# Fused attention and two gated layers on one core: reciprocals through a DRAM scratch, and a reordered gate in layer 1

## The chip, the cores and the metric

The kernel runs on one core of one Trainium2 chip. The metric is the device time of one execution in microseconds (us): the median of several runs of the same kernel. Lower is better.

## The reference

Pooled attention over 4 batches of 8 heads (1152 keys, 576 pooled queries, 64 columns each), then two feed-forward layers of 2304 tokens, 512 → 2048 → 512, each with its own gate:

```python
q_pool = q.reshape(B, H, S // 2, 2, D).mean(axis=3)
scores = scale * q_pool @ k^T;  scores -= max(scores)
attn = exp(scores);  attn = attn / (sum(attn) + 1e-9);  x = attn @ v
h = x @ w_in;   x = (h - tanh(h)) @ w_out           # layer 1
h = x @ w_in2;  out = (h / (1 + exp(-1.702 h))) @ w_out2   # layer 2
```

## The kernel before

Everything is fp32 accuracy from split operands: a value is a rounded high part and a low rest, and each product is three matmuls. The order of the work is written by hand (`tc.manual_schedule()`): every engine and the SP queue, which issues nearly all DMAs, run their instructions in the order in which the program emits them. Three stages follow each other.

**Attention** (`attention`, L185). The heads go in 16 pairs. A pair is 18 passes `i` = 0..17 of the loop over `g` (L479): nine key tiles of one head, then nine of the other. In one pass PE makes the scores `sc` (L320, L321), ACT takes two exponentials (`pf`, `ph`, L322, L324), DVE or POOL subtracts them (`pl`, L333), and PE, three passes later, adds to the output `pv` (L349). L321 needs a row of `q3` with the maxima of its queries. They are made one pair ahead: PE `mx` (L282), DVE reduce (L285), DVE transpose `tt` (L291) and four small DMAs `q<-tt` (L297, `max_rows`, pass 12). `stack` (passes 2 and 12) copies a head's operands in six DMAs, L271 to L276.

A finished head lies in `u` with its row of sums. `sums` (pass 4 of the next pair) brings the sums of a pair to 64 + 64 partitions (`s9`, L363, L365) and moves the second head under the first (L367). `recip` (pass 8): POOL L373, DVE reciprocal L375, then two DMAs (L378) that put the 576 reciprocals into one partition of `rb`, for each head. `spread` (pass 11): two DMAs (L387) copy that partition to the 63 below it. `normalise` (pass 16): DVE multiplies `u` by `rb` into the tokens `xb` (L397).

Weights are loaded to `raw` (L108, two buffers) and converted in three steps (`convert_steps`): s0 is ACT L121 and DVE L122, L126; s1 is DVE L133, L137; the split is ACT L144 and POOL L145. The table `when` (L406) sets the pass of each for the first weights: in the last pair `i` 3 is converted at passes 1, 2 and 4.

**Layers 1 and 2** (`moe`, L525) are 48 steps each: four quarters of the hidden width, six blocks of tokens, two halves `fp`. In step w PE makes `h` (24 matmuls, L550) and then the `y` of step w - 2 (L619); `gate` follows on ACT and DVE. `y` of `fp` 0 needs four PSUM banks, which come free when the previous `y` has been added to `xb`: by ACT copies (L630) in the first quarter, by DVE adds (L632) later, emitted between the gate's DVE operations. At the top of step w, `split_g(w - 1)` copies the gate's result to its high part (ACT L596) and takes the low rest (L598, on POOL in layer 1). Layer 1's gate is a polynomial in u = h² with a tanh branch, and a mask picks one:

```python
u = Square(h) (ACT L566); a = Square(u + GA0) (L567); d = tanh(h) (L568); e = Square(u + GB0) (L569)
g = GC*u*h (DVE L570); u = Relu(u - T2), the mask (ACT L572); d = h - d (DVE L574)
g = (a + GA1)*g (DVE L576); g = (e + GB1)*g (L579); copy d into g where the mask is set (L582)
```

`h` lies in PSUM, where ACT and DVE both read it; such reads of one PSUM tile are kept in the program's order. The table in `moe` (L648) gives the half-step of each later load and conversion.

Of the kernel before, what the change touches and what calls it, by code (L numbers as in the profile page):

```python
# [28 lines left out]
def tile_pooled_attention_two_moe(  # L29
# [31 lines left out]
    wpool = ctx.enter_context(tc.tile_pool(name="wpool", bufs=1))  # L61

# [122 lines left out]
    def attention(ctx: ExitStack):  # L185
# [174 lines left out]
        def sums(p):  # L360
            ua, ub = halves.pop(2 * p), halves.pop(2 * p + 1)
            s9 = wpool.tile([128, QJ], F32, tag="s9", name="s9", bufs=2)
            nc.sync.dma_start(  # L363
                out=s9[0:64, :], in_=ua[64:65, :].rearrange("o (p i) -> o p i", i=QJ))
            nc.sync.dma_start(  # L365
                out=s9[64:128, :], in_=ub[64:65, :].rearrange("o (p i) -> o p i", i=QJ))
            nc.sync.dma_start(out=ua[64:128, :], in_=ub[0:64, :])  # L367
            norm[p] = dict(ua=ua, s9=s9)

        def recip(p):  # L370
            s9 = norm[p]["s9"]
            r9 = wpool.tile([128, QJ], F32, tag="r9", name="r9", bufs=2)
            nc.gpsimd.tensor_scalar(  # L373
                out=r9, in0=s9, scalar1=1.0, scalar2=1e-9, op0=ALU.mult, op1=ALU.add)
            nc.vector.reciprocal(r9, r9)  # L375
            rb = wpool.tile([128, SP], F32, tag="rb", name="rb", bufs=1)
            for s in range(2):
                nc.sync.dma_start(  # L378
                    out=rb[64 * s:64 * s + 1, :].rearrange("o (p i) -> o p i", i=QJ),
                    in_=r9[64 * s:64 * s + 64, :])  # L380
            norm[p]["rb"] = rb

        def spread(p):
            rb = norm[p]["rb"]
            for s in range(2):
                row = rb[64 * s:64 * s + 1, :].unsqueeze(1)
                nc.sync.dma_start(  # L387
                    out=rb[64 * s + 1:64 * s + 64, :], in_=row.to_broadcast([1, 63, SP]))

        def normalise(p):  # L390
# [88 lines left out]
        for g in range(total + LAG):  # L479
# [43 lines left out]
        return lambda: (recip(last), spread(last)), lambda: normalise(last)  # L523

    def moe(ctx: ExitStack, ending):  # L525
# [30 lines left out]
        def gate(n, h, adds):  # L556

            g = temp("gg", 2)

            def add():  # L560
                if adds:
                    adds.pop(0)()

            if steps[n][0] == 0:
                u, a, e, d = temp("u"), temp("a"), temp("e"), temp("d")
                nc.scalar.activation(u, h, AF.Square)  # L566
                nc.scalar.activation(a, u, AF.Square, bias=GA0)  # L567
# [13 lines left out]
                add()
                nc.vector.copy_predicated(g, u[:].bitcast(I32), d)  # L582
            else:
                s = temp("a")
                nc.scalar.activation(s, h, AF.Sigmoid, scale=1.702)  # L585
                add()
                nc.vector.tensor_mul(g, h, s)
            gg[n] = g
            while adds:
                add()  # L590

        def split_g(n):
# [6 lines left out]
            gs[n] = gt  # L599

        def y_part(n):
# [35 lines left out]
            return [lambda m=m: add(m) for m in range(nm)]  # L637
# [24 lines left out]
        for w in range(len(steps) + YLAG):  # L662
            if 0 < w <= len(steps):
                split_g(w - 1)
# [6 lines left out]
            while adds:  # L671
                adds.pop(0)()
# [53 lines left out]
```

## Time and profile before

| what | us |
|---|---|
| median of 3 runs (1485.83 to 1492.15) | 1488.1 |
| the profiled execution | 1484.25 |
| its span, first to last instruction | 1482.4 |
| busy PE / DVE / ACT / POOL | 1343.8 / 1071.7 / 827.6 / 459.1 |

The profile is of one execution, 1.85 us of which lie outside the span. Shares of busy time are averages over three stages with different limits; the waits say more. A busy PE is not PE at its full clock.

### The profile page before, as it was taken

The page shows a single profiled execution, that of the slowest core. Times are in us where ns is not written, and L with a number is a line of the kernel's source. Part 1 is how long each engine was busy: PE and PEld are TensorE (multiplying, and loading weights), DVE is VectorE, ACT ScalarE, POOL GpSimd, SP SyncE. Part 2 cuts the span into 40 slices and gives each one's busy share as a digit, 9 for nine tenths or more (in the row PEclk, how much of TensorE's full clock was granted, in tenths as well). Part 3 has the DMA queues.
Part 4 walks back from the last instruction along what each step waited for, and adds up shares of the span by engine and source line. Part 5 has one row for each costly group of instructions (what it writes and reads, how often), then busy time and mean ns, then how long its engine had stood idle before and what let it go on. Part 6 is the DMA issues. An engine that isn't in the chain of part 4 may idle for free. (4 is left out here: it accounts for less than half of the span.)

```text
span 1482.4 us, 20903 instructions
## 1 busy us (share of the span) xinstructions
PE 1343.8 (91%) x7632; PEld 1262.8 (85%) x7632; DVE 1071.7 (72%) x1230; ACT 827.6 (56%) x1855; POOL 459.1 (31%) x344
## 2 busy tenths in 40 slices
PE   5998988887989797988998888988899999999998
PEld 4998888887989786878988888878899999999997
DVE  6886867777878787799789879889885345554433
ACT  2786767775868676576654555555654332222221
POOL 6554444443545445233322332232211010111000
PEclk9999999998999998999999999999999999999999
DMA  7756666666666564121001100101011101010011
GB/s 200 174 115 139 146 134 146 134 147 133 148 134 147 104 117 104 26 59 44 29 29 43 43 29 29 43 29 43 29 43 57 44 29 57 29 57 29 22 43 64
DMA packets 44038, 117.63 MB, mean 79 GB/s; under 512 B 11968, under 2 KB 11968, under 8 KB 43936
## 3 DMA queue, kind: packets, MB, share of 16 engines
q1 hardware_dynamic: 43900, 116.30, 32.4%
q8 instruction: 60, 0.98, 0.3%
q14 instruction: 42, 0.34, 0.1%
q10 hardware_dynamic: 36, 0.00, 0.0%
HBM read 61.87 MB, written 4.72 MB: 45 GB/s over the span
## 5 line engine op out<-in xcount | busy, mean ns | idle before, releaser
L322 ACT ACTIVATE pf<-sc 128x288 f32<-128x288 f32 x576 | 248.1, 432 | 147.6 <-PE sc L321 130.8
L324 ACT ACTIVATE ph<-sc 128x288 fp32r<-128x288 f32 x564 | 247.1, 438 | 0.0
L333 DVE TENSOR_TENSOR pl<-pf,ph 128x576 fp32r<-128x576 f32 x224 | 207.7, 948 | 41.0 <-ACT ph L324 35.7
L285 DVE TENSOR_REDUCE mt<-mx 128x1 fp32r<-128x1152 f32 x144 | 194.5, 1353 | 41.9 <-PE mx L282 41.7
L321 PE MATMUL sc<-q,a 65*128 65x288 f32 x576 | 172.8, 312 | 39.9 <-DMA q<-tt 39.9
L596 ACT ACTIVATE g<-gg 128x768 fp32r<-128x768 f32 x96 | 81.3, 847 | 209.5 <-DVE gg L582 156.7
L320 PE MATMUL sc<-q,a 128*128 128x288 f32 x576 | 173.6, 312 | 16.2 <-ACT pf L322 9.6
L598 POOL TENSOR_TENSOR g<-gg,g 128x768 fp32r<-128x768 f32 x48 | 91.9, 1916 | 273.3 <-ACT g L596 273.3
L321 PEld LDWEIGHTS sc<-q,a 65*128 65x128 f32 x576 | 115.4, 200 | 42.5 <-issue 32.1
L585 ACT ACTIVATE a<-h 128x768 f32<-128x768 f32 x48 | 39.0, 812 | 199.8 <-PE h L550 199.8
L632 DVE TENSOR_TENSOR xb<-xb,y 128x384 f32<-128x384 f32 (+1 forms) x126 | 76.0, 605 | 103.0 <-PE y L619 103.0
L349 PE MATMUL pv<-pl,vh 128*128 128x288 f32 x576 | 140.9, 309 | 8.2 <-DVE pl L333 4.6
L349 PE MATMUL pv<-ph,vh 128*128 128x288 f32 x576 | 140.9, 309 | 1.7
L349 PE MATMUL pv<-ph,vl 128*128 128x288 f32 x576 | 138.1, 304 | 0.0
L550 PE MATMUL h<-hl,w 128*128 128x384 f32 x720 | 131.4, 336 | 5.0 <-DVE hl L101 4.7
L320 PEld LDWEIGHTS sc<-q,a 128*128 128x128 f32 x576 | 115.5, 200 | 23.8 <-ACT ph L324 11.3
L550 PEld LDWEIGHTS h<-hl,w 128*128 128x128 f32 x720 | 125.6, 188 | 7.8 <-DVE hl L101 6.0
L282 PE MATMUL mx<-kh,bdq 128*128 128x384 f32 x432 | 112.8, 375 | 16.9 <-DVE mt L285 9.8
L333 POOL TENSOR_TENSOR pl<-pf,ph 128x576 fp32r<-128x576 f32 x64 | 103.6, 1618 | 63.1 <-ACT ph L324 52.3
L619 PE MATMUL y<-g,w 128*128 128x384 f32 x360 | 88.6, 355 | 23.5 <-DVE xb L632 15.2
L349 PEld LDWEIGHTS pv<-pl,vh 128*128 128x128 f32 x576 | 100.3, 198 | 11.1 <-DVE pl L333 5.7
L349 PEld LDWEIGHTS pv<-ph,vh 128*128 128x128 f32 x576 | 104.9, 200 | 5.2 <-ACT u L355 5.0
(114 smaller groups left out, 2908.4 us busy)
## 6 DMA issues: line engine op xcount, KB each, us to landing
a<-kh SPq DMA_DIRECT2D x64, 288.0 KB
raw<-in_moe_w_in_dram SPq DMA_DIRECT2D x32, 512.0 KB
raw<-in_moe_w_out_dram SPq DMA_DIRECT2D x32, 512.0 KB
qr<-in_q_dram SPq DMA_DIRECT2D x16, 576.0 KB
kr<-in_k_dram SPq DMA_DIRECT2D x16, 576.0 KB
vr<-in_v_dram SPq DMA_DIRECT2D x16, 576.0 KB
q<-qh SPq DMA_DIRECT2D x64, 144.0 KB
a<-kl SPq DMA_DIRECT2D x32, 288.0 KB
```

The costliest lines, as they stand in the source:

```text
L282: nc.tensor.matmul(mx[:, a, 0:384], bdqs[p % 2][:, j, :], d["kh"][:, a * 384:(a + 1) * 384], start=True, stop=True)
L285: nc.vector.tensor_reduce(d["mt"][:, j:j + 1], mx[:, :, 0:384], AX.XY, ALU.max, negate=True)
L320: nc.tensor.matmul(sc, a1[:, ks], q2[:, xs], start=True, stop=False)
L321: nc.tensor.matmul(sc, a2[:, ks], q3[:, xs], start=False, stop=True)
L322: nc.scalar.activation(pf[:, xs], sc, AF.Exp, scale=SCALE)
L324: nc.scalar.activation(ph[:, xs], sc, AF.Exp, scale=SCALE)
L333: eng.tensor_tensor(pl, pf, f32(ph[:]), op=ALU.subtract)
L349: nc.tensor.matmul(accs[hd][x], w[:, t, :], r[:, x * HB:(x + 1) * HB], start=(t == 0 and n == 0), stop=(t == KT - 1 and n == 2))
L550: nc.tensor.matmul(hb[:, j, 0:TB], wi[:, c, w, :], x[r][c], start=(k == 0), stop=(k == 3 * NKC - 1))
L596: nc.scalar.activation(gt[:, :, 0, :], g, AF.Copy)
L598: eng.tensor_tensor(gt[:, :, 1, :], g, f32(gt[:, :, 0, :]), op=ALU.subtract)
L619: nc.tensor.matmul(ys[m][:, 0:w], lhsT, rhs, start=(fp == 0 and k == 0), stop=(fp == 1 and k == 5))
```

## The change

In attention the second head is moved (now `merge`, pass 9) after the reciprocals; these go to a DRAM tile `rd` in one DMA; `spread` (pass 15) reads 64 + 64 rows back from DRAM, each row all 576 values; `normalise` comes in pass 2 of the pair after. The conversions of `i` 3, `o` 1, `o` 2 and `o` 3 in the last pair come three or four passes later. In layer 1 the first product is emitted ahead of tanh, the second ahead of the subtraction; the copy of the last step's result (`split_g`) stands behind the square; the mask goes to `a` instead of `u`; the adds are spread anew. The later conversions have new half-steps.

```diff
 def sums(p):
-            nc.sync.dma_start(out=ua[64:128, :], in_=ub[0:64, :])
...
 def recip(p):
             nc.vector.reciprocal(r9, r9)
-            for s in range(2):
-                nc.sync.dma_start(out=rb[64 * s:64 * s + 1, :]..., in_=r9[64 * s:64 * s + 64, :])
+        def merge(p):
+            nc.sync.dma_start(out=d["ua"][64:128, :], in_=d["ub"][0:64, :])
+            d["rd"] = drpool.tile([128, QJ], F32, tag="rd", name="rd", bufs=2)
+            nc.sync.dma_start(out=d["rd"], in_=d["r9"])
 def spread(p):
             for s in range(2):
-                row = rb[64 * s:64 * s + 1, :].unsqueeze(1)
-                nc.sync.dma_start(out=rb[64 * s + 1:64 * s + 64, :], in_=row.to_broadcast([1, 63, SP]))
+                r = slice(64 * s, 64 * s + 64)
+                row = d["rd"][r, :].rearrange("p i -> (p i)").unsqueeze(0)
+                nc.sync.dma_start(out=d["rb"][r, :], in_=row.to_broadcast([64, SP]))
...
-            ("i", 3, (-2, 14), (-1, 1), (-1, 2), (-1, 4)),
+            ("i", 3, (-2, 14), (-1, 4), (-1, 5), (-1, 7)),
...
-                elif i == 11:
+                elif i == 9:
+                    merge(p - 1)
+                elif i == 15:
                     spread(p - 1)
-                elif i == 16:
-                    normalise(p - 1)
+            if p > 1 and i == 2:
+                normalise(p - 2)
...
 def gate(n, h, adds):
                 nc.scalar.activation(u, h, AF.Square)
+                if n > 0:
+                    split_g(n - 1)
                 nc.scalar.activation(a, u, AF.Square, bias=GA0)
-                nc.scalar.activation(d, h, AF.Tanh)
-                nc.scalar.activation(e, u, AF.Square, bias=GB0)
                 nc.vector.scalar_tensor_tensor(out=g, in0=u, scalar=GC, in1=h, ...)
-                nc.scalar.activation(u, u, AF.Relu, bias=-T2)
                 add()
+                nc.vector.scalar_tensor_tensor(out=g, in0=a, scalar=GA1, in1=g, ...)
+                add(True)
+                nc.scalar.activation(d, h, AF.Tanh)
+                add(True)
+                nc.scalar.activation(e, u, AF.Square, bias=GB0)
+                add(True)
+                add()
                 nc.vector.tensor_sub(d, h, d)
                 add()
-                nc.vector.scalar_tensor_tensor(out=g, in0=a, scalar=GA1, in1=g, ...)
-                add()
+                nc.scalar.activation(a, u, AF.Relu, bias=-T2)
                 nc.vector.scalar_tensor_tensor(out=g, in0=e, scalar=GB1, in1=g, ...)
                 add()
-                nc.vector.copy_predicated(g, u[:].bitcast(I32), d)
+                nc.vector.copy_predicated(g, a[:].bitcast(I32), d)
...
-                ("i", 0, 1, 5, 6, 7), ("i", 1, 4, 8, 9, 10), ("o", 0, 7, 11, 12, 13),
-                ("o", 1, 10, 13, 14, 15), ("i", 2, 13, 16, 17, 21), ("i", 3, 15, 18, 19, 22),
-                ("o", 2, 18, 23, 24, 27), ("o", 3, 20, 25, 26, 28),
+                ("i", 0, 1, 5, 5, 6), ("o", 1, 3, 7, 8, 10), ("i", 1, 5, 9, 9, 10),
+                ("o", 0, 8, 13, 13, 14), ("i", 2, 10, 15, 16, 21), ("i", 3, 13, 17, 17, 22),
+                ("o", 2, 17, 23, 24, 26), ("o", 3, 19, 25, 27, 28),
```

`add(True)` takes an ACT copy of the first quarter, `add()` a DVE add. After attention, `normalise` of the last pair but one, the last reciprocals and their DMA stand at half-step 1, `spread` at 3 and the last `normalise` at 7 (before: 3 and 8). Below `moe`, line numbers of the changed kernel are 9 to 15 higher.

The SP queue in one pair of attention (`s`: sums, `r`: reciprocals, `a` and `q`: a head's operands), first before:

```order
L367 DMA u<-u 64x576
L214 DMA qr<-in_q_dram 128x1152
L218 DMA kr<-in_k_dram 128x1152
L378 DMA rb<-r_1391 1x64x9 x2
L387 DMA rb<-rb 63x1x576 x2
L297 DMA q_0_88<-tt 1x9x32 x2
L297 DMA q_1_91<-tt 1x9x32 x2
L271 DMA a_1_71<-kh 64x1152
L272 DMA q_1_90<-qh 64x576
L273 DMA a_1_71<-kl 64x1152
L274 DMA q_1_90<-qh 64x576
L275 DMA a_1_89<-kh 64x1152
```

and in the change:

```order
L380 DMA u<-u 64x576
L382 DMA rd<-r_1392 128x9
L298 DMA q_0_90<-tt 1x9x32 x2
L298 DMA q_1_93<-tt 1x9x32 x2
L272 DMA a_1_73<-kh 64x1152
L273 DMA q_1_92<-qh 64x576
L274 DMA a_1_73<-kl 64x1152
L275 DMA q_1_92<-qh 64x576
L276 DMA a_1_91<-kh 64x1152
L277 DMA q_1_93<-ql 64x576
L223 DMA vr<-in_v_dram 128x1152
L390 DMA rb<-rd 64x576 x2
```

The spread of `rb` has moved from ahead of the four `q<-tt` to behind them, the next head's six copies and a load.

DVE in one step of layer 1 with adds, before:

```order
L570 SCALAR_TENSOR_TENSOR gg<-u,h 128x768
L632 TENSOR_TENSOR xb_65<-xb_65,y 128x384
L574 TENSOR_TENSOR d<-h,d 128x768
L632 TENSOR_TENSOR xb_65<-xb_65,y 128x384
L576 SCALAR_TENSOR_TENSOR gg<-a,gg 128x768
L632 TENSOR_TENSOR xb_65<-xb_65,y 128x384
L579 SCALAR_TENSOR_TENSOR gg<-e,gg 128x768
L632 TENSOR_TENSOR xb_65<-xb_65,y 128x384
L582 COPY_PREDICATED gg<-u,d 128x768
```

and in the change:

```order
L585 SCALAR_TENSOR_TENSOR gg<-u,h 128x768
L644 TENSOR_TENSOR xb_67<-xb_67,y 128x384
L588 SCALAR_TENSOR_TENSOR gg<-a,gg 128x768
L644 TENSOR_TENSOR xb_67<-xb_67,y 128x384
L596 TENSOR_TENSOR d<-h,d 128x768
L644 TENSOR_TENSOR xb_67<-xb_67,y 128x384
L599 SCALAR_TENSOR_TENSOR gg<-e,gg 128x768
L644 TENSOR_TENSOR xb_67<-xb_67,y 128x384
L602 COPY_PREDICATED gg<-a,d 128x768
```

The product with `a` now stands ahead of the subtraction that needs tanh.

ACT between two steps of layer 1, before:

```order
L566 ACTIVATE u<-h 128x768
L567 ACTIVATE a<-u 128x768
L568 ACTIVATE d<-h 128x768
L569 ACTIVATE e<-u 128x768
L572 ACTIVATE u<-u 128x768
L144 ACTIVATE vl_77<-wt 128x512
L596 ACTIVATE g<-gg 128x2x384
L144 ACTIVATE w_7752<-wt 128x512
L566 ACTIVATE u<-h 128x768
```

and in the change:

```order
L581 ACTIVATE u<-h 128x768
L566 ACTIVATE g<-gg 128x2x384
L584 ACTIVATE a<-u 128x768
L591 ACTIVATE d<-h 128x768
L593 ACTIVATE e<-u 128x768
L598 ACTIVATE a<-u 128x768
L145 ACTIVATE w_7753<-wt 128x512
L581 ACTIVATE u<-h 128x768
L566 ACTIVATE g<-gg 128x2x384
```

The copy `g<-gg`, which waits for the last gate's end on DVE, has moved from ahead of the next square to behind it.

## Rows read from the trace of the kernel before

**Rows 1.** Windows by stage: length; busy us (instructions) PE, PEld, DVE, ACT, POOL; clock; DMA share; GB/s
```profile
92.40:555.60 463.20, 410.06 (x2688) 395.05 (x2686) 361.28 (x390) 340.39 (x1032) 211.49 (x171) 0.94 0.65 137
601.50:1069.00 467.50, 417.07 (x2257) 396.67 (x2257) 395.13 (x452) 273.70 (x397) 130.31 (x76) 0.98 0.12 38
1069.00:1482.00 413.00, 408.13 (x2065) 370.96 (x2064) 210.08 (x281) 130.47 (x189) 41.12 (x29) 1.00 0.13 43
```
**Rows 2.** Waits of PE in attention (60 to 600 us): us, times, longest
```profile
PE sc L321 <- DMA q<-tt: 38.0, 11, 5.7
...
PE mx L282 <- DVE mt L285: 7.2, 5, 2.6
```
**Rows 3.** Waits of the whole span
```profile
DVE gg L570 <- ACT d L568: 37.9, 15, 4.2
PE y L619 <- DVE xb L632: 37.3, 22, 3.2
```
**Rows 4.** Timeline of DVE and PE at one pair's end: start, us, instruction, idle before
```profile
258.19 0.20 DVE L291 STREAM_TRANSPOSE tt<-mt 128x32 f32<-128x32 f32 x1
...
272.00 0.58 PE L321 MATMUL sc<-q,a 65*128 65x288 f32 x1 [3.51 <-DMA q<-tt]
272.03 0.83 DVE L397 TENSOR_TENSOR xb<-u,rb 128x192 f32<-128x192 f32 x2 [2.95 <-DMA q<-tt]
```
**Rows 5.** Timeline of the SP queue at the same pair's end
```profile
260.52 1.63 SPq L387 DMA_DIRECT2D rb<-rb  x2
262.24 9.33 SPq L297 DMA_DIRECT2D q<-tt  x4
```
**Rows 6.** Windows while loads move, and while the spread moves (columns of group 1)
```profile
256.00:259.00 3.00, 3.00 (x23) 2.81 (x22) 2.00 (x4) 2.82 (x10) 0.60 (x2) 1.00 0.98 346
262.00:270.00 8.00, 6.49 (x47) 6.25 (x46) 7.08 (x8) 5.57 (x18) 0.47 (x1) 1.00 0.46 34
```
**Rows 7.** Windows of pairs 1 and 10, first score to first score
```profile
62.50:92.40 29.90, 29.64 (x209) 28.79 (x208) 24.80 (x28) 25.92 (x80) 13.06 (x11) 1.00 0.50 112
...
381.10:412.50 31.40, 30.14 (x209) 28.89 (x208) 26.93 (x30) 26.01 (x80) 17.85 (x14) 1.00 0.74 169
```
**Rows 8.** Groups by line in layer 1, whole, then quarter 2: busy, mean ns, idle before
```profile
L570 DVE SCALAR_TENSOR_TENSOR gg<-u,h 128x768 f32<-128x768 f32 x48 | 45.6, 950 | 56.6 <-ACT d L568 37.9 <-POOL g L598 7.7 <-PE h L550 3.8
...
L570 DVE SCALAR_TENSOR_TENSOR gg<-u,h 128x768 f32<-128x768 f32 x12 | 11.4, 950 | 18.4 <-ACT d L568 15.3 <-POOL bdq L145 3.0
```
**Rows 9.** Timeline of DVE between two gates, with no conversion between them
```profile
828.26 0.95 DVE L570 SCALAR_TENSOR_TENSOR gg<-u,h 128x768 f32<-128x768 f32 x1 [3.83 <-ACT d L568]
```
**Rows 10.** Issues of DMAs, KB of one
```profile
a<-kh SPq DMA_DIRECT2D x64, 288.0 KB
...
q<-qh SPq DMA_DIRECT2D x64, 144.0 KB
```
**Rows 11.** Timeline of ACT in the last pair: a conversion waits for its load
```profile
566.05 0.68 ACT L121 ACTIVATE wa<-raw 128x512 f32<-128x512 f32 x1 [6.85 <-DMA raw<-in_moe_w_in_dram]
```
**Rows 12.** Windows of quarter 2 of layer 1, and of one of its steps
```profile
709.30:823.80 114.50, 105.56 (x578) 100.53 (x577) 94.27 (x108) 67.08 (x96) 33.58 (x20) 0.99 0.12 37
...
718.90:727.20 8.30, 8.30 (x49) 8.30 (x49) 8.02 (x9) 4.57 (x7) 1.18 (x1) 1.00 0.21 63
```
**Rows 13.** Timeline of ACT, POOL and DVE between two gates, with a conversion
```profile
834.75 0.85 ACT L596 ACTIVATE g<-gg 128x768 fp32r<-128x768 f32 x1 [4.03 <-DVE gg L582]
...
835.67 1.85 POOL L598 TENSOR_TENSOR g<-gg,g 128x768 fp32r<-128x768 f32 x1 [7.13 <-ACT g L596]
835.78 2.29 DVE L133 SCALAR_TENSOR_TENSOR wt<-wa,wt 128x512 f32<-128x512 f32 x1
```
**Rows 14.** Timeline of DVE a little later
```profile
870.51 1.92 DVE L576 SCALAR_TENSOR_TENSOR gg<-a,gg 128x768 f32<-128x768 f32 x1
...
880.82 0.95 DVE L576 SCALAR_TENSOR_TENSOR gg<-a,gg 128x768 f32<-128x768 f32 x1
...
883.89 0.67 DVE L133 SCALAR_TENSOR_TENSOR wt<-wa,wt 128x512 f32<-128x512 f32 x1
```

More of the change, by code (lines that the diff above doesn't have):

```diff
@@ L61, in tile_pooled_attention_two_moe @@
     wpool = ctx.enter_context(tc.tile_pool(name="wpool", bufs=1))
+    drpool = ctx.enter_context(tc.tile_pool(name="drpool", bufs=1, space=bass.MemoryType.DRAM))
     xb = [xpool.tile([128, NKC, TB], F32, name=f"xb{i}") for i in range(NB)]
@@ L366, in sums @@
                 out=s9[64:128, :], in_=ub[64:65, :].rearrange("o (p i) -> o p i", i=QJ))
-            nc.sync.dma_start(out=ua[64:128, :], in_=ub[0:64, :])
-            norm[p] = dict(ua=ua, s9=s9)
+            norm[p] = dict(ua=ua, ub=ub, s9=s9)
         def recip(p):
@@ L375, in recip, with spread @@
             nc.vector.reciprocal(r9, r9)
-            rb = wpool.tile([128, SP], F32, tag="rb", name="rb", bufs=1)
-            for s in range(2):
[L378 to L384, printed above, removed]
-            for s in range(2):
-                row = rb[64 * s:64 * s + 1, :].unsqueeze(1)
-                nc.sync.dma_start(
-                    out=rb[64 * s + 1:64 * s + 64, :], in_=row.to_broadcast([1, 63, SP]))
+            norm[p]["r9"] = r9
+        def merge(p):
+            d = norm[p]
+            nc.sync.dma_start(out=d["ua"][64:128, :], in_=d["ub"][0:64, :])
+            d["rd"] = drpool.tile([128, QJ], F32, tag="rd", name="rd", bufs=2)
+            nc.sync.dma_start(out=d["rd"], in_=d["r9"])
+        def spread(p):
+            d = norm[p]
+            d["rb"] = wpool.tile([128, SP], F32, tag="rb", name="rb", bufs=1)
+            for s in range(2):
+                r = slice(64 * s, 64 * s + 64)
+                row = d["rd"][r, :].rearrange("p i -> (p i)").unsqueeze(0)
+                nc.sync.dma_start(out=d["rb"][r, :], in_=row.to_broadcast([64, SP]))
         def normalise(p):
@@ L522, in attention @@
         sums(last)
-        return lambda: (recip(last), spread(last)), lambda: normalise(last)
+        return (
+            lambda: (normalise(last - 1), recip(last), merge(last)),
+            lambda: spread(last), lambda: normalise(last))
     def moe(ctx: ExitStack, ending):
@@ L599, in split_g, with gate, add @@
             gs[n] = gt
+        def gate(n, h, adds):
+            g = temp("gg", 2)
+            def add(scalar=False):
+                if adds and adds[0][0] is scalar:
+                    adds.pop(0)[1]()
+            if steps[n][0] == 0:
+                u, a, e, d = temp("u"), temp("a"), temp("e"), temp("d")
+                nc.scalar.activation(u, h, AF.Square)
+                if n > 0:
+                    split_g(n - 1)
+                nc.scalar.activation(a, u, AF.Square, bias=GA0)
+                nc.vector.scalar_tensor_tensor(
+                    out=g, in0=u, scalar=GC, in1=h, op0=ALU.mult, op1=ALU.mult)
+                add()
+                nc.vector.scalar_tensor_tensor(
+                    out=g, in0=a, scalar=GA1, in1=g, op0=ALU.add, op1=ALU.mult)
+                add(True)
[3 more added lines that the diff above has]
+                add(True)
+                add()
+                nc.vector.tensor_sub(d, h, d)
+                add()
+                nc.scalar.activation(a, u, AF.Relu, bias=-T2)
+                nc.vector.scalar_tensor_tensor(
+                    out=g, in0=e, scalar=GB1, in1=g, op0=ALU.add, op1=ALU.mult)
+                add()
+                nc.vector.copy_predicated(g, a[:].bitcast(I32), d)
+            else:
+                split_g(n - 1)
+                s = temp("a")
+                nc.scalar.activation(s, h, AF.Sigmoid, scale=1.702)
+                add()
+                nc.vector.tensor_mul(g, h, s)
+            gg[n] = g
+            while adds:
+                adds.pop(0)[1]()
         def y_part(n):
@@ L635, in add @@
                     nc.sync.dma_start(out=out[r0:r0 + 128, :], in_=dst)
-            return [lambda m=m: add(m) for m in range(nm)]
+            return [(qq == 0, lambda m=m: add(m)) for m in range(nm)]
         later = {}
@@ L642, in at @@
             later.setdefault(slot, []).append(job)
-        at(3, ending[0])
-        at(8, ending[1])
+        at(1, ending[0])
+        at(3, ending[1])
+        at(7, ending[2])
         per = 4 * NB
@@ L662, in moe @@
         for w in range(len(steps) + YLAG):
-            if 0 < w <= len(steps):
+            if w == len(steps):
                 split_g(w - 1)
@@ L671, in moe @@
             while adds:
-                adds.pop(0)()
+                adds.pop(0)[1]()
             for go in later.pop(2 * w + 1, ()):
```

27 lines of the change are left out of this document (removed), and 6 rows, old and new, of the table when.

## The prediction

> **What bounds the kernel now.** I read the windows by stage first [rows 1]: PE is busy 408.1 of 413.0 us in layer 2 at full clock, so nothing that the change does there can be seen; in attention it is busy 410.1 of 463.2 us at a mean clock of 0.94, and in layer 1 417.1 of 467.5 us. Both stages have time to give. The lists of waits say where it goes: in attention PE waits 38.0 us for the small DMAs `q<-tt` [rows 2], in layer 1 DVE waits 37.9 us for tanh (`d`), and PE 37.3 us for DVE's adds [rows 3].
>
> The wait in attention is read at one pair's end. DVE has the transposed maxima at 258.2 [rows 4], but SP does not issue them: it first waits for the reciprocals' rows to land, issues the spread of `rb` from 260.5 on, and then needs 9.3 us for four small DMAs [rows 5]. PE reaches the first score that wants `q3` and stands 3.5 us; DVE stands 2.95 us at `normalise`, for the same moment [rows 4]. While the spread moves, 34 GB/s flow at a DMA share of 0.46; just before, loads from DRAM flow at 346 GB/s and 0.98 [rows 6]. So the small DMAs stand behind a slow copy out of one partition. And the clock is 0.94 over the stage [rows 1] where pairs without such a wait have 1.00 [rows 7].
>
> In layer 1 the chain is on DVE. Between two gates with no conversion between them, DVE's first product starts 3.83 us after the last gate's end, when tanh has ended on ACT [rows 9], though it needs only u and h. Over the layer L570 has 56.6 us of idle time ahead of it [rows 8]; it delays every add behind it, and for those PE waits.
>
> **The change, part by part.** *Ends of pairs.* The spread goes behind the `q<-tt`, and the rows that it waited for leave SP's queue. The four DMAs can then issue at about 258.3, with only loads that already move ahead of them, ten microseconds before PE wants them. What leaves is 38.0 us of waits [rows 2] and the low clock after them: a mean of 0.94 over 463.2 us is 56 us at 1.2 GHz in the place of 2.4, and half of that, 28 us, is lost; I give 22 of it to these waits. Together 60. Checked by pairs: 463.2 us for 13 pairs is 35.6 each; pair 1, without the wait, takes 29.9 with PE busy 29.64, and pair 10, likewise without, 31.4 [rows 7]. At 30.0 each, plus 7.2 us for `mt` that stay [rows 2] and some 12 for smaller waits and restarts (what pair 10 has above pair 1, 1.5 us, in eight pairs), 13 pairs take 409: a gain of **54**. Bounds: 60, if nothing comes in its place; and 13 x 31.4 + 7.2 + 6 = 421, a gain of 42, if every pair is like the slower row. I stay nearer to pair 1, since pair 10 carries the tail of a weight conversion.
>
> *What is added there.* One write of 4.6 KB to DRAM in the place of two small DMAs, and 2 x 64 rows in the place of 2 x 63. Behind the spread now stand the next head's `stack` copies, which have most of a pair to land. `rd` waits on SP for the reciprocal, as L378 did; behind it stand the `q<-tt`, whose transposition comes later on DVE anyway. `merge` no longer waits for the sums. `normalise` costs its 0.83 us [rows 4] as before. How fast one row comes out of DRAM 64 times no row shows: bounds for 2 x 147 KB are the loads' 346 GB/s, 0.9 us, and the spread's own 34, 8.7 us [rows 6]. `normalise` stands five passes, about 8 us, behind the issue, with a head's copies ahead in the queues. I take the first and call it hidden; the other is a rival.
>
> *The last pair.* ACT, and PE behind it, wait 6.85 us for `raw` at pass 1 [rows 11]. The conversion comes three passes later and its load is issued earlier. Gain **6**, bounds 0 and 7.
>
> *Layer 1, the gate.* If DVE starts its first product when the last gate ends, 56.6 us of idle time go [rows 8]. Three things give some back. PE's own step is 8.3 us [rows 12], so twelve of them cannot go below 99.6: the second quarter has 18.4 us of this idle time [rows 8] but can give only 114.5 - 99.6 = 14.9, so 3.5 less. Second, the new second product waits for ACT, which first copies the last result (0.85 [rows 13]) and makes `a` (about as long), against 0.95 for the first product: 0.75 us in some 8 steps that have neither adds nor conversions between, 6 us. Third, DVE and POOL collide. POOL's subtraction starts right behind the copy and takes 1.85 us, and the DVE operation beside it takes 2.29 us [rows 13], where alone it takes 0.67; L576 takes 1.92 or 0.95 [rows 14]. Until now that subtraction falls into DVE's idle time wherever there is any; from now on it meets the second product. Such idle waits are about 22 (15 at a mean of 2.5 us in [rows 3]; 56.6 at that mean are 22), and each meeting costs the 1.0 us of [rows 14]: 21 us. That leaves 56.6 - 3.5 - 6 - 21 = **26**. Bounds: without collisions and waits 53; with 12 more conversions in collision (2.29 - 0.67 = 1.6 us each, 19 us) 7.
>
> The Trainium skill (SBUF — State Buffer, Who interferes with whom) says that a DVE operation with two SBUF inputs and a POOL operation that reads SBUF share a port, and the one that issues second waits for the whole of the first. L133's 2.29 us, ending 0.5 us after the subtraction's end, agrees. By the rule at its worst each of the 22 would wait 1.85 us, 41 us, and layer 1 would gain 6.
>
> *Adds, mask, conversions.* The mask's other tile lets the next square run before the last gate ends, without which the first product could not start early; by itself it costs nothing. The high part now waits on ACT for the next `h`. It is due when PE has made one more `h`, most of a step later, and that covers the copy and POOL's 1.85 us; without this cover each step would grow by what is missing. The respread conversions are the same work. A step in which DVE is busy 8.02 us passes in 8.30 [rows 12], so a step with its share of them fits. After attention the last `rb` is off every path as long as it lands within three steps.
>
> **Sum.** 1484.25 - 54 - 6 - 26 = 1398 for the profiled execution (span 1482.4). The median before stands 3.85 above it, so the forecast is **1402**.
>
> **Rivals.** *Slower: the spread is as slow out of DRAM.* It then moves 8.7 us, behind its own issue (1.6 us [rows 5]) and a head's copies (3 x 288 and 3 x 144 KB [rows 10], 3.8 us at 346 GB/s): 14 us after pass 15, where DVE comes to `normalise` after 8. DVE then stands 6 us, ahead of the reduces that PE's maxima need; a pair of 30 us has 3 us of DVE slack (26.9 busy [rows 7]), so 14 x 3 = 42 us come back, and the time is 1444. If the copies of the next head, waiting on PE, share the engines at the spread's 34 GB/s for another 6 us, 14 x 9 = 126 come back, and it is 1528. Slower than before begins at 86 / 14 + 3 = 9.1 us of wait a pair. For it: the row of 34 GB/s. Against: the loads' row, whose source is DRAM, as here. The slower case 4 in 100; the milder is in the next.
>
> The Trainium skill (DMA: Bandwidth & Descriptors, Why a DMA increments its semaphore by 16 and not by 1) says that a DMA runs on the largest number of engines, up to 16, that divides its outer sizes: 9 for 63 rows, 16 for 64. The share of 0.46, 7.4 engines, does not speak against it. By that rule the same packets would take 9/16 of the 8.7 us, and DVE's wait would be 2 us, inside its slack.
>
> *The wait only moves in attention*: DVE stands at `normalise` as above, or PE still at `q<-tt`, because the transposition itself is late once pairs are shorter. Of 54 us some 20 stay: 1402 + 34 = 1436. For it: DVE's 26.9 busy us in a pair of 30 leave little. 10 in 100.
>
> *Layer 1 gives nothing*, because collisions eat the 53 us: that takes 1.1 us in each of 48 steps, and one L576 costs 1.0 [rows 14]. 1402 + 26 = 1428. 14 in 100.
>
> *The change does not do what it says*: something else holds the `q<-tt`, and only layer 1 and the last pair gain: 1402 + 54 = 1456. Against it: 9.3 us for four tiny issues right behind the spread [rows 5]. 4 in 100.
>
> **How the numbers follow.** The forecast has 68 in 100. Its bounds together, gains of 60 + 7 + 53 = 120 and 42 + 0 + 7 = 49, give 1368 and 1439. That range takes in 1428 and 1436 and leaves out 1456 and the slower case, 8 in 100, and what lies beyond the bounds. A measurement of this kernel tells about 0.5% from no change, 7.4 us: faster than 1480.7 are all but the slower case and a remnant of the mild ones, 0.94; within 0.02; slower 0.04.
>
> **What would show it.** In the profile after: PE's wait for `q<-tt` under 8 us; pairs of 30 to 31.4 us; a clock near 1.00 in attention; the four `q<-tt` issued within some 3 us; idle time ahead of the first product under 15 us; the second product at 1.5 us or more in the mean. Wrong, if DVE waits for `rb<-rd` by more than 3 us a pair, if quarter 2 of layer 1 stays above 110 us, or if PE waits for `g` from POOL.

## The result, and the profile after

The changed kernel takes 1429.5 us (median of 4 runs, 1425.82 to 1433.14) against 1487.0 for the kernel before, a ratio of 0.9595 with a 95% interval of 0.956 to 0.963. The forecast was 1402 in a range of 1368 to 1439: the side and the range hold, but the gain is 57 us where 86 were worked out. The profiled execution takes 1433.14 us, span 1431.4.

The windows by stage of the changed kernel, with the columns of [rows 1]: attention from pair 2 to the end of pair 14, layer 1, layer 2.

```profile
93.80:530.60 436.80, 395.21 (x2688) 379.12 (x2687) 382.38 (x391) 340.02 (x1032) 217.26 (x171) 0.99 0.57 144
574.40:1020.50 446.10, 417.13 (x2257) 404.87 (x2257) 403.83 (x457) 271.58 (x401) 133.10 (x77) 0.96 0.13 39
1020.50:1431.00 410.50, 407.08 (x2066) 371.15 (x2064) 217.13 (x279) 127.11 (x184) 37.69 (x29) 1.00 0.13 43
```

Against [rows 1] attention lost 26.4 us and layer 1 21.4, and 2.6 more in the step that hands over to layer 2 (10.91 to 8.32); pair 15 with the way to layer 1 went from 45.9 to 43.8. What lies before pair 2 took 1.4 us longer. Together 51 us between the two profiled executions.

The longest of PE's waits in the changed attention (60 to 572 us), then its issues of `q<-tt`, and one VectorE and GpSimd stretch at pass 2 to 4 of pair 6 (timeline: start, us, instruction, idle before):

```profile
PE mx L283 <- DVE mt L286: 38.1, 30, 3.0
```
```profile
214.66 3.08 SPq L298 DMA_DIRECT2D q<-tt  x4
```
```profile
230.28 1.34 DVE L286 TENSOR_REDUCE mt<-mx 128x1 fp32r<-128x1152 f32 x1
231.55 0.74 DVE L334 TENSOR_TENSOR pl<-pf,ph 128x576 fp32r<-128x576 f32 x1
232.22 2.52 DVE L399 TENSOR_TENSOR xb<-u,rb 128x192 f32<-128x192 f32 x2
234.66 1.34 DVE L286 TENSOR_REDUCE mt<-mx 128x1 fp32r<-128x1152 f32 x1
...
231.57 2.01 POOL L334 TENSOR_TENSOR pl<-pf,ph 128x576 fp32r<-128x576 f32 x1 [4.43 <-ACT ph L325]
233.55 0.78 POOL L303 TENSOR_SCALAR vh<-vr 128x576 fp32r<-128x576 f32 x1
...
236.06 0.79 PE L283 MATMUL mx<-kh,bdq 128*128 128x384 f32 x3 [1.40 <-DVE mt L286]
```

The 38.0 us for `q<-tt` [rows 2] are gone from this list, and the four DMAs issue in 3.08 us where they took 9.33 [rows 5]. In their place PE waits 38.1 us for `mt`, the reduce of the maxima, where it waited 7.2 [rows 2]. The timeline says why at one place: `normalise` takes 2.52 us where it took 0.83 [rows 4]. Its first product starts while GpSimd's subtraction of 2.01 us runs, its second runs beside GpSimd's next operation (L303, on the values), and the reduce behind it, and PE's next `mx`, come late. Two operations that run at once in this way, and of which one takes longer for it, are called a meeting or a collision below. From first score to first score pairs 3 to 8 take 32.5 us each (pair 6 33.0), not 30; pass 4 is 3.6 us long where pair 1, which has no `normalise`, has 2.1.

Layer 1, VectorE by line, changed kernel (busy, mean ns, idle before):

```profile
L588 DVE SCALAR_TENSOR_TENSOR gg<-a,gg 128x768 f32<-128x768 f32 x47 | 72.5, 1543 | 9.5 <-ACT a L584 7.4
...
L585 DVE SCALAR_TENSOR_TENSOR gg<-u,h 128x768 f32<-128x768 f32 x48 | 45.5, 948 | 19.5 <-ACT u L581 19.5
...
L599 DVE SCALAR_TENSOR_TENSOR gg<-e,gg 128x768 f32<-128x768 f32 x47 | 44.4, 945 | 0.1
L134 DVE SCALAR_TENSOR_TENSOR wt<-wa,wt 128x512 f32<-128x512 f32 x30 | 39.7, 1325 | 2.6
```

and in the kernel before, the second product, the third and the conversions:

```profile
L576 DVE SCALAR_TENSOR_TENSOR gg<-a,gg 128x768 f32<-128x768 f32 x47 | 52.4, 1114 | 0.0
L579 DVE SCALAR_TENSOR_TENSOR gg<-e,gg 128x768 f32<-128x768 f32 x47 | 52.1, 1109 | 3.2
...
L133 DVE SCALAR_TENSOR_TENSOR wt<-wa,wt 128x512 f32<-128x512 f32 x30 | 49.0, 1635 | 1.9 <-DVE wt L126 0.5
```

The idle time ahead of the first product fell from 56.6 [rows 8] to 19.5; none of it is for tanh. The second product has a mean of 1.54 us where it had 1.11, on its way from 0.95 to the 1.92 of [rows 14]. The third product and the conversions got shorter, so VectorE's busy time in the layer rose by 8.7 us only, from 395.1 [rows 1] to 403.8.

### The profile page after: what moved, and what is told of

Read it like the earlier page. It is cut to its first block, busy times and chain, and to the rows that moved or that the text cites. A ratio compares the mean times of both kernels' runs of the same rounds, so it can differ in the third digit from the quotient of the medians.

```text
span 1431.4 us, 20817 instructions
## 1 busy us (share of the span) xinstructions
PE 1329.1 (93%) x7632; PEld 1256.1 (88%) x7632; DVE 1107.9 (77%) x1232; ACT 821.9 (57%) x1855; POOL 463.8 (32%) x344
## 4 chain that ended last, share of the span: by engine, by line
PE 33%; DVE 18%; ACT 5%; issue 4%; DVEq 0%; ACTq 0%
PE y L631 17%; PE h L556 16%; DVE gg L588 4%; DVE gg L602 3%; DVE wt L134 3%; DVE gg L599 2%; DVE gg L585 2%; DVE wt L127 2%; ACT g L566 1%; DVE d L596 1%; ACT a L584 1%; DVE hl L102 1%; DVE wt L123 1%; DVE wt L138 1%; DVE xb L644 1%
## 5 line engine op out<-in xcount | busy, mean ns | idle before, releaser
L334 DVE TENSOR_TENSOR pl<-pf,ph 128x576 fp32r<-128x576 f32 x224 | 202.7, 922 | 36.0 <-ACT ph L325 35.9
L321 PE MATMUL sc<-q,a 128*128 128x288 f32 x576 | 169.2, 306 | 9.2 <-ACT pf L323 3.4
L322 PE MATMUL sc<-q,a 65*128 65x288 f32 x576 | 167.6, 303 | 2.0 <-DMA q<-tt 2.0
L556 PE MATMUL h<-hl,w 128*128 128x384 f32 x720 | 134.6, 342 | 8.4 <-DVE hl L102 8.4
L350 PE MATMUL pv<-ph,vh 128*128 128x288 f32 x576 | 137.9, 303 | 1.7
L556 PEld LDWEIGHTS h<-hl,w 128*128 128x128 f32 x720 | 129.2, 193 | 10.6 <-DVE hl L102 9.3
L283 PEld LDWEIGHTS mx<-kh,bdq 128*128 128x128 f32 x432 | 76.4, 204 | 60.2 <-DVE mt L286 53.2
L322 PEld LDWEIGHTS sc<-q,a 65*128 65x128 f32 x576 | 112.2, 195 | 2.3 <-issue 2.3
L556 PE MATMUL h<-hl,bdq 128*128 128x384 f32 x600 | 108.3, 335 | 0.0
```

What stands on the lines that cost most here:

```text
L283: nc.tensor.matmul(mx[:, a, 0:384], bdqs[p % 2][:, j, :], d["kh"][:, a * 384:(a + 1) * 384], start=True, stop=True)
L321: nc.tensor.matmul(sc, a1[:, ks], q2[:, xs], start=True, stop=False)
L322: nc.tensor.matmul(sc, a2[:, ks], q3[:, xs], start=False, stop=True)
L334: eng.tensor_tensor(pl, pf, f32(ph[:]), op=ALU.subtract)
L350: nc.tensor.matmul(accs[hd][x], w[:, t, :], r[:, x * HB:(x + 1) * HB], start=(t == 0 and n == 0), stop=(t == KT - 1 and n == 2))
L556: nc.tensor.matmul(hb[:, j, 0:TB], wi[:, c, w, :], x[r][c], start=(k == 0), stop=(k == 3 * NKC - 1))
```

## The experiments

Three questions: do the parts add; what holds attention's pairs at 32.5 us; what did layer 1 gain and lose. Each run changes the changed kernel unless it says otherwise.

**The parts alone.** `attn_only` is the changed kernel with layer 1 of before, `gate_only` the kernel before with layer 1 of the change.

> The changed attention (reciprocals through DRAM, merge at pass 9, spread at 15, normalise at pass 2 a pair later, moved conversions of pairs 13 to 15) with layer 1 as it was. If the two parts of the change do not touch each other, this keeps what the two traces show for attention: pairs 2 to 14 shorter by 26 us and pair 15 with its end by 2 us, so 28 us off, about 1459 us. The rival is that the part in layer 1 also pays for itself through the attention's end (an earlier end leaves conversions and last normalise out of its way): then this run comes out nearer to 1470.

> The changed order of layer 1 (second Square and copy of g ahead of tanh, first product early, mask in a's tile, conversions respread) with attention as it was. Theory: 21 us in the first layer and 2.5 us in the step that hands over to the second, so 24 us off, about 1463 us, and the wait of the first product for tanh falls from 57 to 20 us as in the changed kernel. Rival: part of the 24 us comes from attention's end having moved, then 1470 or more.

Measured: 1454.0 us, ratio 0.9765 (0.9738 to 0.9792), and 1462.0 us, 0.9816 (0.9797 to 0.9835). What they take off, 0.0235 and 0.0184, adds to 0.042; both together took off 0.0405, so within the intervals the parts are independent, and neither rival holds. By their profiled executions they gain 30 and 22 us.

**Where `normalise` stands.**

```diff
-            if p > 1 and i == 2:
+            if 1 < p < NPAIR and i == 10:
                 normalise(p - 2)
```

> The changed kernel with the two products of normalise moved from pass 2 to pass 10 of the same pair, where GpSimd subtracts nothing and no maximum is reduced; no work added or removed. Theory (placement: at pass 2 the normalise meets GpSimd's subtraction, takes 2.6 us instead of 0.9 and makes the reduce that TensorE's next maxima wait for late): a normalise takes 0.9 us again, pass 4 of a pair falls from 3.6 to about 2.1 us, pairs 2 to 14 lose 1.3 to 1.7 us each, so 17 to 22 us off: about 1410 us. Rival 1 (VectorE is simply full over a pair, wherever the work stands): pairs stay at 32.5 us, 1429 us. Rival 2 (the trip through DRAM lands too late): only pairs 10, 12 and 14, where VectorE waits 3 times and 9.8 us for the spread, get shorter, 1420 us.

Measured: 1416.1 us, ratio 0.9515 (0.9489 to 0.954). Pass 4 fell to 1.9 us, pairs 3 to 8 to 30.8 to 31.3. Rival 1 falls for these pairs, and rival 2 does too, since they had no wait for the spread; pairs 10 and 12 got shorter as well (35.8 to 31.5 and 36.7 to 31.9). The work is not quite the same: the changed kernel normalises the last pair but one twice, with the same result (34 products in its trace, 32 here), and this run once. In the profile of this run (waits of PE, pairs 2 to 14):

```profile
PE mx L283 <- DVE mt L286: 15.2, 17, 1.5
...
PE pv L350 <- ACT u L356: 6.3, 2, 3.1
```

The second row is a new wait: pairs 9 and 11, which carry weight conversions, got longer (39.3 and 36.9), because there the late `normalise` still holds a `u` that ACT wants at pass 11.

**The other pair of operations that meet.** As before, and:

```diff
-            (2, 11): [(prep_kh, 1)], (2, 14): [(prep_ql,), (load_v,)],
+            (2, 11): [(prep_kh, 1), (prep_ql,)], (2, 14): [(load_v,)],
-            (3, 16): [(prep_qs,)],
+            (3, 13): [(prep_qs,)],
```

> As the run before it, and the low rest of the queries at pass 11 in place of 14 and the sum of the queries' two halves at pass 13 in place of 16, away from GpSimd's two subtractions of the keys' low rest at passes 16 and 17. Theory (placement): the sum takes 0.75 us in place of 1.4, the reduces of passes 16 to 1 come earlier, pass 1 of a pair falls from 2.9 to about 1.9 us: another 13 us off, about 1397 us. Rival (what holds pass 1 is GpSimd's or ScalarE's lateness at a pair's end, not VectorE's): no difference from the run before it.

Measured: 1403.1 us, ratio 0.9418 (0.9396 to 0.944). Pass 1 fell from 3.1 us (pairs 3 to 8 of `norm10`) to 1.9, and a regular pair takes what the prediction gave it:

```profile
214.70:244.50 29.80, 29.53 (x210) 28.87 (x209) 26.06 (x30) 26.05 (x81) 16.47 (x14) 1.00 0.64 166
```

That row is the window of pair 6 (columns of [rows 1]): 29.8 us, PE busy 29.53, as in pair 1 [rows 7]. But the meeting did not go. At a pair's start GpSimd subtracts for the keys (L264), and VectorE's `qs` and `pl` run beside it (`norm10`, then this run):

```profile
250.18 3.33 POOL L264 TENSOR_TENSOR kl<-kr,kh 128x576 fp32r<-128x576 f32 x2 [4.77 <-DMA a<-kl]
251.31 0.92 DVE L234 TENSOR_TENSOR qs<-qr 128x576 f32<-128x576 f32 x1
252.14 1.99 DVE L334 TENSOR_TENSOR pl<-pf,ph 128x576 fp32r<-128x576 f32 x1
```
```profile
244.36 3.34 POOL L264 TENSOR_TENSOR kl<-kr,kh 128x576 fp32r<-128x576 f32 x2 [5.47 <-DMA a<-kl]
244.64 1.77 DVE L334 TENSOR_TENSOR pl<-pf,ph 128x576 fp32r<-128x576 f32 x1
```

A `pl` of 0.74 us still takes 1.44 to 1.77 here in pairs 3 to 8, against 1.98 to 1.99 in `norm10`. So the move of `qs` and `ql` pays 13 us; how much of that is the meeting, and how much the shorter queue ahead of the reduces, no run separates.

**Place, or collision?** Moving an operation changes both. `pool_fill2` leaves `normalise` at pass 2 and takes the reads away from the subtraction beside it; `no_meet` also moves GpSimd's work on the values.

```diff
+            if g % NS == 2 and g < (NPAIR - 1) * NS:
+                eng.memset(f32(pl[:]), 0.0)
+            else:
                 eng.tensor_tensor(pl, pf, f32(ph[:]), op=ALU.subtract)
...
-                elif i == 3:
+                elif i == 7:
                     prep_v(n, 0)
```

> The changed kernel with normalise still at pass 2, but GpSimd's subtraction that stands beside it (the low rest of the probabilities of pass 2 of each pair but the last) is a fill with zeros, which reads nothing: this part of the computation is left out. Theory (the two products collide with a GpSimd subtraction that reads two SBUF tiles): a normalise takes 0.9 us in place of 2.6, pass 4 of a pair falls from 3.6 to about 2.1 us, pairs 3 to 8 take 31 us in place of 32.5, about 1412 us. Rival (not the collision but the place: two more operations between two reduces make the reduce late by themselves): pass 4 stays over 3.2 us, pairs over 32 us.

Measured: 1431.1 us, pass 4 3.4 us, pairs 32.3. That would speak for the rival, had the collision gone. It had not (timeline of this run):

```profile
229.93 1.81 POOL L306 TENSOR_TENSOR vl<-vr,vh 128x576 fp32r<-128x576 f32 x1
230.37 2.05 DVE L402 TENSOR_TENSOR xb<-u,rb 128x192 f32<-128x192 f32 x2
```

GpSimd, free sooner, started its subtraction for the values 0.44 us before the first product. So the next run moved that one too (last two lines of the diff).

> The run with the zero fill again (the low rest of the probabilities of pass 2 of each pair but the last is left out), and GpSimd's two operations on the values, which stood at pass 3 and met the first product there, moved to pass 7. Normalise stays at pass 2 and now has no subtraction of GpSimd beside it. Theory 1 (the collision is the cause): normalise takes 0.9 us and pass 4 falls to 2.2 us or less, pairs 4 to 8 to 31.0 us. Theory 2 (the place alone is the cause): normalise takes 0.9 us, pass 4 stays over 3.0 us. Both have a part if pass 4 comes out between.

Measured: 1408.8 us. The timeline of VectorE:

```profile
226.57 0.81 DVE L402 TENSOR_TENSOR xb<-u,rb 128x192 f32<-128x192 f32 x2
227.31 1.35 DVE L286 TENSOR_REDUCE mt<-mx 128x1 fp32r<-128x1152 f32 x1
```

Still at pass 2, `normalise` takes 0.81 us, pass 4 is 1.9 us, and pairs 3 to 8 take 30.8 to 31.0 us but for one of 31.6: all that the move to pass 10 gave. So for `normalise` the collision is the cause, and the place matters only through it. (Both of these runs were timed once.) The Trainium skill (SBUF — State Buffer, Who interferes with whom) says that such a pair shares a read port, and that the second to issue waits for the whole of the first. The rows agree: in the changed kernel GpSimd's subtraction ends at 233.58, and the first product, 1.58 us long where both together take 0.81 above, at 233.80.

**The trip through DRAM.** The reciprocals go through a row of `rb`, as before the change, at the new places.

```diff
 def merge(p):
-            d["rd"] = drpool.tile([128, QJ], F32, tag="rd", name="rd", bufs=2)
-            nc.sync.dma_start(out=d["rd"], in_=d["r9"])
+            for s in range(2):
+                nc.sync.dma_start(out=rb[64 * s:64 * s + 1, :]..., in_=d["r9"][64 * s:64 * s + 64, :])
 def spread(p):
-                nc.sync.dma_start(out=d["rb"][r, :], in_=row.to_broadcast([64, SP]))
+                nc.sync.dma_start(out=rb[64 * s + 1:64 * s + 64, :], in_=row.to_broadcast([1, 63, SP]))
```

> The changed kernel, but the reciprocals go to one row of rb at pass 9 and from there to the other 63 rows at pass 15, all in SBUF, as the kernel before did it; the places of all else are those of the changed kernel. Theory (what took the 38 us of waits away is the place, pass 15 in place of 11, behind the rows of maxima and not ahead of them): q<-tt still issues in 3 us and TensorE's wait for it stays near 0; the slow copy, some 8 us in the kernel before, lands about at normalise's place, so VectorE waits up to 3 us a pair for it: between 1429 and 1455 us. Rival (the trip through DRAM itself took them away, since the copy out of one partition slows every other transfer beside it wherever it stands): the rows of stack at passes 2 and 12 become late, TensorE waits for q or a rows 2 us or more a pair, and the attention's 26 us are lost whole, 1456 us or more.

Measured: 1473.9 us, ratio 0.9897 (0.9866 to 0.9928): 44 us above the changed kernel, all of it in pairs 2 to 14 (482.7 us against 436.8). The place alone does take PE's wait for `q<-tt` away: none is left, and the four issue in 3.1 us. Otherwise the rival holds in size, but not by its way: no wait of PE for `q` or `a` rows shows; VectorE waits ahead of `normalise`, in 13 places for 51 us together (the last rows below; "issue" means that the profile names nothing that ended the wait), and the reduce behind it is late again. SP's queue behind the two kinds of spread (changed kernel, then this run), the data rate behind the slow one, its wait, and all VectorE's waits there (pairs 2 to 14):

```profile
224.37 1.38 SPq L390 DMA_DIRECT2D rb<-rd  x2
225.85 0.54 SPq L272 DMA_DIRECT2D a<-kh  x1
226.43 0.59 SPq L273 DMA_DIRECT2D q<-qh  x1
```
```profile
276.85 1.59 SPq L392 DMA_DIRECT2D rb<-rb  x2
278.55 3.86 SPq L272 DMA_DIRECT2D a<-kh  x1
282.45 4.33 SPq L273 DMA_DIRECT2D q<-qh  x1
```
```profile
280.00:283.00 3.00, 2.27 (x16) 2.03 (x15) 3.00 (x4) 1.41 (x6) 0.00 (x0) 1.00 0.52 60
284.00:287.00 3.00, 2.84 (x19) 2.56 (x19) 0.47 (x1) 3.00 (x10) 2.92 (x3) 1.00 0.47 55
```
```profile
288.28 0.83 DVE L402 TENSOR_TENSOR xb<-u,rb 128x192 f32<-128x192 f32 x2 [3.81 <-DMA rb<-rb]
```
```profile
DVE xb L402 <- issue: 29.9, 7, 6.5
DVE xb L402 <- DMA rb<-rb: 13.6, 4, 3.8
DVE xb L402 <- DMA q<-qh: 7.6, 2, 3.9
```

The rate is 55 to 60 GB/s for some 7 us, and the next two issues take 3.9 and 4.3 us, not 0.6; in all 13 of these pairs the first takes 3.6 to 4.0. Over the changed kernel's spread and the copies behind it 255 GB/s flow (window 225 to 229 us). So the new places alone do not pay: with the slow spread these pairs take 482.7 us, 19.5 more than before the change [rows 1], and what is left of the gain is layer 1's. The fast spread is what makes them pay. Whether its source does it, or the 64 rows in place of 63, was not separated.

**Layer 1: GpSimd's subtraction.** First without its reads, then on VectorE.

```diff
+            if li == 0:
+                eng.memset(f32(gt[:, :, 1, :]), 0.0)
```

> The changed kernel, but in layer 1 GpSimd fills the low rest of g with zeros in place of subtracting it, so that it reads nothing: this part of the computation is left out. Theory (the copy of g and the subtraction behind it now start while VectorE makes the second product, which collides with it): the second product falls from 1.54 us to about 0.95 and VectorE's products all fall; VectorE is what layer 1 waits for, so quarters 2 to 4 lose 20 to 40 us together (1.0 us of a collision a step, 16 steps a... 48 steps in all) and the total comes to 1390 to 1410 us. Rival (VectorE has slack there, the steps wait for ScalarE's chain of Square, tanh and Square): the second product is shorter but the steps are not, over 1420 us.

Measured, once: 1382.9 us, layer 1 397.7 us, with PE busy for 394.8 of them: 48 us of layer 1 hang on what this subtraction reads. The window of layer 1, and VectorE by line in it:

```profile
572.30:970.00 397.70, 394.77 (x2257) 390.72 (x2257) 352.45 (x456) 268.30 (x401) 78.18 (x78) 1.00 0.14 44
```
```profile
L591 DVE SCALAR_TENSOR_TENSOR gg<-a,gg 128x768 f32<-128x768 f32 x47 | 45.0, 958 | 10.7 <-ACT a L587 8.3
...
L134 DVE SCALAR_TENSOR_TENSOR wt<-wa,wt 128x512 f32<-128x512 f32 x30 | 20.7, 690 | 3.0 <-DVE wt L127 0.5
```

The second product lost 27.5 us of VectorE's time and the conversions' L134 19.0, together 46.5. In `low_dve` the subtraction is computed, on VectorE:

```diff
                     out=g, in0=u, scalar=GC, in1=h, op0=ALU.mult, op1=ALU.mult)
+                if low:
+                    low()
```

> The changed kernel, but layer 1's low rest of g is subtracted by VectorE, right behind the first product of the next step, and not by GpSimd; nothing is left out. VectorE gets 47 operations of about 0.95 us more, 11.4 us a quarter. Theory (the subtraction on GpSimd costs VectorE's second product and the conversions beside it as much as it would cost VectorE itself, and with it TensorE's steps wait): with the quarter's busy time of VectorE of the run that left the subtraction out, 84 to 95 us, plus 11.4, the first three quarters come to TensorE's floor of 100 and the last to 106: 405 to 410 us of layer 1 in place of 446, about 1392 us. Rival (VectorE's work is the bound however it is shared: 45 us more work against 47 us of collisions): no change, 1425 to 1432 us.

Measured: 1405.1 us, ratio 0.9426 (0.94 to 0.9453). The rival falls; the theory was 13 us too good, layer 1 being 418.3 us and not 405 to 410:

```profile
576.60:994.90 418.30, 403.57 (x2259) 389.37 (x2258) 386.56 (x503) 272.55 (x402) 48.26 (x31) 1.00 0.13 42
```

VectorE is busy for 386.6 us in place of 403.8, with 44 us of subtractions added. With the old table of conversions too, in `all` below, the layer takes 405.3.

**Layer 1: the respread conversions**, put back to the table of before:

> The changed kernel with layer 1's table of weight conversions put back to that of before; all else changed. If the order of the gate (products and copies) gave the 24 us of layer 1 and the respread tables nothing, this is 1429 us. If the respread did a part, as the few long steps of 12 to 15 us with conversions in both kernels suggest, it is 1432 to 1440 us. Were the table worth as much as the gate's order, 1441 us.

Measured: 1418.1 us, ratio 0.9504 (0.9476 to 0.9531), outside every case: the new table costs 11 us. Layer 1 is 429.9 us, 16 less, and the handing step 1.8 more. The window of layer 1 and two of VectorE's lines in this run:

```profile
575.30:1005.20 429.90, 408.63 (x2258) 396.60 (x2257) 405.25 (x454) 269.58 (x399) 135.83 (x76) 0.98 0.13 41
```
```profile
L588 DVE SCALAR_TENSOR_TENSOR gg<-a,gg 128x768 f32<-128x768 f32 x47 | 65.0, 1383 | 7.4 <-ACT a L584 4.2 <-DVE gg L585 0.5
...
L585 DVE SCALAR_TENSOR_TENSOR gg<-u,h 128x768 f32<-128x768 f32 x47 | 44.5, 947 | 6.7 <-ACT u L581 6.7
```

In the changed kernel a long step stands between two of PE's shortest (windows, columns of [rows 1]):

```profile
723.00:731.30 8.30, 8.30 (x50) 8.30 (x49) 8.02 (x9) 3.89 (x6) 2.68 (x2) 1.00 0.21 66
731.30:744.50 13.20, 10.66 (x50) 9.80 (x49) 11.20 (x13) 7.01 (x10) 4.29 (x4) 0.87 0.13 40
744.50:752.90 8.40, 8.40 (x50) 8.40 (x50) 7.16 (x8) 3.74 (x6) 1.64 (x1) 1.00 0.00 0
```

The middle step holds both halves of a conversion and four adds, 11.2 us of VectorE, and what it overruns the neighbours cannot give back. It holds a wait, too: ACT splits the converted weight (L145) as soon as VectorE's L138 ends, ahead of the square, and the first product waits 1.47 us for that. The trace has this ten times in the changed kernel and twice in `old_conv`, which is most of the 19.5 us of idle time against 6.7. The clock takes its part: for the same matmuls PE is busy for 417.1 us at a mean clock of 0.96 with the new table and 408.6 at 0.98 with the old one, 8.5 of the 16 us. I read the table's cost there; no run moved one conversion alone.

**What paid, together.** `both` is `norm10_qs13` with the old table; `all` adds the subtraction on VectorE, `normalise` at pass 9, and conversions of pairs 8 to 13 in halves:

```diff
-            ("i", 0, (-8, 6), (-7, 5), (-7, 8), (-7, 16)),
-            ("i", 1, (-6, 6), (-5, 5), (-5, 8), (-5, 16)),
-            ("o", 0, (-4, 6), (-3, 5), (-3, 8), (-3, 16)),
+            ("i", 0, (-9, 6), (-8, 14), (-7, 14), (-7, 17)),
+            ("i", 1, (-7, 6), (-6, 14), (-5, 14), (-5, 17)),
+            ("o", 0, (-5, 6), (-4, 14), (-3, 14), (-3, 17)),
```

> The two placements that paid, together: normalise at pass 10, the queries' low rest at pass 11, their sum at pass 13, and layer 1's old table of conversions; all else as changed. If the gains lie in different stages they add: 26 us and 11 us off the changed kernel, about 1392 us. Rival: layer 1's gain with the old table came from where attention ended, then 1400 us or more.

> As the run before it (normalise at pass 9, one pass earlier), with the low rest of g on VectorE, and the three weight pieces that are converted in pairs 9 to 14 taken in halves, one half a pair, at pass 14 where no maximum is reduced, from pair 8 on. Theory: layer 1 at 405 to 410 us in place of 446, pairs 9, 11 and 13 at 31 us in place of 34.5 to 36: 1403 less 36 to 40 less 9 to 12, so 1351 to 1358 us. Rival 1 (with the low rest on VectorE the old table makes it late again): layer 1 at 420 us, 1370 us. Rival 2 (a half conversion of 2.6 us a pair at pass 14 makes the reduces of passes 15 and 16 late in six pairs): pairs 8 to 13 at 32 us or more each, 1360 us or more.

Measured: 1389.5 us, ratio 0.9338 (0.9317 to 0.9359), so the gains add; and 1350.9 us, ratio 0.9076 (0.9061 to 0.9091), which beats both kernels. Its windows of pairs 2 to 14 and of layer 1:

```profile
93.30:489.00 395.70, 386.67 (x2687) 374.23 (x2686) 348.90 (x390) 340.14 (x1032) 219.37 (x171) 1.00 0.63 159
531.30:936.60 405.30, 397.69 (x2257) 390.09 (x2257) 388.54 (x500) 273.04 (x399) 46.65 (x31) 1.00 0.14 43
```

No pair of these is over 31.6 us, and PE is busy for 98% of both stretches.

## Why the prediction was right, and where its steps failed

- **Ends of pairs, 54 (42 to 60): measured 26**, below its own lower bound. That the total still lies in the stated range is luck: the range adds all the lower bounds, and layer 1 gave 24 where its lower bound was 7. What the term said of the wait held: the four issues in 3 us, no PE wait for `q<-tt`, the clock at 0.99. The step that failed is "`normalise` costs its 0.83 us as before": it cost 2.5 at its new place. A second meeting came with the change: GpSimd's subtraction for the keys, which began 5 us or more into a pair before, now runs beside `qs` (1.37 us in the mean) or the `pl` behind it. The moves of `normalise` and of `qs` took 13 us each off the time (1429.5 to 1416.1 to 1403.1). With both, pairs 2 to 14 take 407.5 us where the prediction had 409, and a regular pair 29.8 where it had 30.0. For `normalise` the cause is shown, and clearing its collision in place took 21 us; for `qs` only the place. Conversion pairs 9, 11 and 13, for which the sum allowed some 31.5 us each, still take 34.5 to 36.1 there; in `all` they take 30.3 to 30.9.
- **DVE's lateness** stood among the rivals as 1436 (the wait only moves), and that is about what happened, though at another operation, PE's `mx`, and through collisions rather than the fullness that was given for it: the 26.1 busy us of VectorE in a pair of `norm10_qs13` fit into 29.8; in the changed kernel pair 6 has 28.4.
- **The spread out of DRAM, hidden:** right but for three pairs, in which VectorE waits for `rb`, 9.8 us in all, 6.8 of them in the last pair. The milder price of the slow case, 42 us, is near what `sbuf_spread` costs, 44. The rule on the number of engines (the Trainium skill, DMA: Bandwidth & Descriptors, Why a DMA increments its semaphore by 16 and not by 1) stays open: shares of 0.47 and 0.52 do not speak against nine engines of 16, but no run here tells rows from source.
- **The last pair, 6 (0 to 7): measured 2.** The wait for `raw` fell from 6.85 us [rows 11] to 2.50 and moved to pass 6. There VectorE also waits for `rb`, and the pass takes 6.6 us:

```profile
540.29 0.66 ACT L122 ACTIVATE wa<-raw 128x512 f32<-128x512 f32 x1 [2.50 <-DMA raw<-in_moe_w_in_dram]
...
541.39 1.32 DVE L399 TENSOR_TENSOR xb<-u,rb 128x192 f32<-128x192 f32 x2 [6.77 <-DMA rb<-rd]
```

- **Layer 1, 26 (7 to 53): measured 24**, by two errors that cancel, so the match is luck. The order of the gate is worth 38 (467.5 to 429.9 in `old_conv`, and 0.8 in the handing step), 12 more than given. "The respread conversions are the same work" was priced at nothing and cost 14 of it (16.2 less the 1.8). A step in which VectorE is busy for 8.02 us does pass in 8.30, as the prediction read; the new table makes steps of 11.2.
- **Collisions in layer 1, 21 in the second product: measured 20** (72.5 us against 52.4), but the term that was subtracted was too large. With the order of the gate alone (`old_conv`) the second product gains 12.6 us (65.0), and VectorE's busy time in the layer 10.1 (395.1 to 405.3): 11 less than the 21, about the 12 by which the order was undervalued. And the whole collision is 48: the forecast charged only what the change adds; what was there already was the larger opportunity.
- **The signs named:** seen were `q<-tt` under 8 us (2.0), the clock, the issues and the second product's mean; missed were pairs of 30 to 31.4 (32.5) and under 15 us ahead of the first product (19.5; 6.7 with the old table). Of those that would prove it wrong two occurred, both small: PE waits for `g` from GpSimd, 4.1 us in all, and in one pair VectorE waits for `rb` by more than 3 us (6.8).

## What to carry to other kernels

When an operation with two SBUF inputs is moved on VectorE, look up what GpSimd does at its new place, and at what moves because a wait left: the price is set by the partner, not by the operation's own row. When a wait is removed, what it kept apart may meet; undo the meetings one at a time, and check in the trace that the meeting is gone before reading the time. A table that moves work without adding any is not free where each step has a floor: look at the longest steps, not the mean, and at what stands behind a moved operation in each engine's order.

## What was not expected of the hardware

Taking the reads away from one GpSimd operation gave nothing, since the next one came forward into the same collision (1431.1), and only clearing both gave 21 us (1408.8). VectorE did 44 us more of work in layer 1 (46 operations of 0.956 us) and the kernel was 24 us faster, because the same subtraction on GpSimd held VectorE for longer than VectorE needs to do it: its busy time in the layer fell from 403.8 to 386.6 us. And behind a copy from one SBUF row to 63 others the next two DMAs issue seven times as long as behind the spread from DRAM, 3.86 and 4.33 us against 0.54 and 0.59.
